# A state-space attention with a gated feed-forward network on one core: wider chunks for the first two pairs, another norm, state additions among the outputs, and a new order of steps

## The chip, the cores and the metric

The kernel runs on one core of one Trainium2 chip. The core has five engines that each work through their own instructions in order and wait for one another by semaphores: TensorE (PE, matrix products; PEld is its loading of weights), VectorE (DVE), ScalarE (ACT), GpSimd (POOL) and SyncE (SP, which here only issues DMA transfers). TensorE reads SBUF and writes PSUM, whose banks the other engines read and free. The metric is the device time of one execution in microseconds (us). All times below are in us.

## The reference

Two operators follow each other. The first is a Mamba-2 state-space scan over x (4 batches, 8 heads, 768 steps, 32 values a head), with a decay a per head and step and with B and C of 16 values. Per head it is a recurrence over chunks of the sequence:

```
log_a = log(clip(a, 1e-6, 1));  cum = cumsum(log_a) within a chunk
L[i,j] = exp(cum[i] - cum[j]) for i >= j, else 0
y      = (C B^T * L) x  +  (C state) * exp(cum)
state  = exp(sum log_a) * state + sum_j exp(cum[-1] - cum[j]) * B_j x_j
```

The result doesn't depend on how long a chunk is, only the work does: the first term of y is inside a chunk (intra-chunk), the second comes from the state before it (inter-chunk).

The heads are put side by side, 3072 tokens of 256 values, and go through the second operator, a feed-forward network without bias:

```
xn  = x / sqrt(mean(x*x) + 1e-6) * rms_g
out = (silu(xn @ w_gate) * (xn @ w_val)) @ w_out        # 256 -> 1536 -> 256
```

All inputs are float32 arrays, and the products are float32 products.

## The kernel before, in words

**Tiling.** The 3072 tokens are six blocks of 512 (numbered 0 to 5). A block is two pairs, so pairs 0 to 11; a pair is two pieces of 128 steps of one batch, in which the scan is worked in chunks of 64, that is four chunks a pair. `NPAIR` is 12, `HC` is 64 (half a piece), `NH` the 8 heads, `NQ` the 4 groups of two heads, `halves` the two chunks of a piece.

**The scan of a pair.** Its steps, by their names in the order and the lines of before.py:

- `bc` and `x` (SP) fetch B, C and x; `scale` (DVE, L449) multiplies them by decays; `turn` (PE, L464) transposes, and `T`, `Tt` (ACT, for pair 0 DVE, L486 and L967 to L970) copy the transposed tiles out of PSUM.
- the decay matrix L: for pairs 0 to 3 `mask`, `sums` (PE, L392 to L409) add the logs up in a pair of PSUM banks and `exp` (ACT, L416) takes the exponential of all 8 heads at once; for later pairs `spread` (SP, L422) writes rows of logs into L by DMA, `sub` (DVE, L428) and `ex` (ACT L434, POOL L436) do the rest. The rows come from `r` (PE, L331) and `parts` (DVE, L338 to L345).
- `g` (PE, L494) is the product of B and C, `L`, `L1` (DVE, L513, L519) multiply it into the decay matrix.
- `A` (PE, L534) is the sum over j in the update of the state, the *additions*; `S` (DVE, L547 to L557) masks them and runs the states on.
- `y` (PE, L574) is the output: the inter-chunk products first, then 64 intra-chunk ones. The result lies in a pair of banks and two single ones, 128 of 512 columns each.
- `sq` (ACT L610, POOL L613) squares it and adds the two halves of features, `yt` (ACT L624, for block 0 DVE L626) copies it out.

**The norm of a block.** `ms` (PE, L636) takes the mean of the squares over features, four small products that leave the tokens on partitions; `mc` (ACT, L642) copies, `mt` (PE, L645) transposes, `rs` (DVE L650, POOL L652) adds 1e-6 and takes the power -1/2, `rb` (PE, L658) transposes four times, so that each token's factor stands on all partitions, and `xn` (DVE, L670, for block 0 L674) multiplies. In block 0 `rc` (ACT, L663) copies the factors to SBUF as `r`.

**The network.** Block 0 begins with plain products: `early` (PE, L703) works on the outputs before they are normed, `norm` (DVE, L714) multiplies by r; `gate` (PE, L693) works on xn; `silu`, `hid` follow, `o` (PE, L809) is the output projection. The rest, from feature tiles 3 to 5 of block 0 on, is done by Strassen's scheme with seven products instead of eight: `P.k.j` (PE, L777, four matmuls of 128x256, 0.86 of PE) is product k of feature tile j, `take` (ACT, L783) copies one of them out of PSUM, `C` (DVE, L789) adds, `silug`, `hidg` or `silu`, `hid` (ACT L798, DVE L802) make the hidden values, `s`, `s2` to `s4` their sums, `O.k.j` (PE, L867) the seven products of the output projection, `Otake` (ACT, L883) and `Oadd` (DVE, L891, L894) combine them, `out` (SP) writes them.

**The weights** come as words of 64-bit floats and are decoded on the core in 20 pieces: `fetch` (SP), `pow` (ACT, L169 to L172), `man` (DVE, L179, L182), `wt` (DVE, L188); `cw`, `tx`, `two` (DVE, L747, L754, L823) make the sums of weights and inputs for Strassen's scheme. Most of that goes on while blocks 0 and 1 are worked.

**What sets the order.** Nothing is scheduled by a program: a string (L1046 to L1207) lists every step as `block:step.numbers/slot`, and a loop (L1208 to L1217) emits the steps in that order. Each step appends its instructions to the engines that it uses, so an engine's queue is the order of the string cut down to that engine, SP's DMA issues and table loads of ACT included. `/slot` names which of three pairs of PSUM banks block 0 uses; `switch` hands two of these over to the network's tiles. `table` asks for an ACT table ahead of its first use. `spread` of a pair needs its L buffer free; there are four (`LBUFS`).

## Time and profile before

| What | us |
|---|---|
| time of the runs, median of 3 | 415.13 (414.54 to 415.45) |
| time of the profiled execution | 414.91 |
| its span, first to last instruction | 413.2 |
| PE busy | 403.3 (98%) |
| DVE busy | 301.0 (73%) |
| ACT busy | 214.8 (52%) |
| POOL busy | 42.3 (10%) |
| mean granted clock of TensorE | 0.996 of full |

The span is what the profile shows; 1.7 of the profiled execution lie around it. "Busy" counts an instruction from its start to its modelled end, and matmuls overlap, so the start of one to the start of the next says what one costs. The parts of the page used below: shares of busy time; the span in 40 slices (a digit is the busy share in tenths); the chain of work that ended last, followed back from the last instruction; groups of instructions by line, operation and tile; the timeline, where consecutive instructions of a kind are put together ("x4"); and busy time by stretch. In a group's or timeline's line `out<-in` names the tiles, and `<-` in the part on idle time names what ended it.

### The profile page before, as it was taken

Reading aid. Unit: us, or ns where it says so; the run is one execution under the profiler, and the core shown is the slowest. Engines: PE = TensorE matmul, PEld = TensorE weight load, DVE = VectorE, ACT = ScalarE, POOL = GpSimd, SP = SyncE. Lnnn points to the kernel's source line nnn. Section 1 sums busy time; section 2 is a strip of 40 time slices with the busy share of each in tenths; the row PEclk is TensorE's granted clock in tenths of the full one; section 3 lists DMA queues with packets and bytes.
Section 4 is the critical chain, followed back from the end, with each engine's and each line's share of the span. In section 5 each row is a group of like instructions: output and inputs, shape, how many; then the busy total and the mean of one; then the engine's idle time right before and its main releaser. Section 6 shows DMA issues by size and latency. Waiting matters only on the chain.

```text
span 413.2 us, 10058 instructions
## 1 busy us (share of the span) xinstructions
PE 403.3 (98%) x4118; PEld 343.2 (83%) x4118; DVE 301.0 (73%) x712; ACT 214.8 (52%) x497; POOL 42.3 (10%) x64
## 2 busy tenths in 40 slices
PE   7789999999999999999999999999999999999997
PEld 5457467888888899888899888899988889988897
DVE  5989999789968878476796465787366876356781
ACT  2869997755656426645362547451556431235410
POOL 2011000012300015000033000012200001000000
PEclk9989999999999999999999999999999999999999
DMA  9979848900111440201070406000100000100001
GB/s 121 255 157 238 208 53 173 203 0 2 39 39 52 92 65 27 78 0 29 12 85 10 78 2 127 2 2 2 52 0 3 1 3 0 52 0 2 1 2 51
DMA packets 87374, 23.95 MB, mean 58 GB/s; under 512 B 76800, under 2 KB 81152, under 8 KB 87328
## 3 DMA queue, kind: packets, MB, share of 16 engines
q1 hardware_dynamic: 83168, 23.05, 26.9%
q10 hardware_dynamic: 4160, 0.26, 1.1%
q8 instruction: 32, 0.52, 0.5%
q14 instruction: 14, 0.11, 0.1%
HBM read 20.02 MB, written 3.28 MB: 56 GB/s over the span
## 4 chain that ended last, share of the span: by engine, by line
PE 90%; DVE 6%; issue 2%; ACT 1%; POOL 0%; DVEq 0%; POOLq 0%
PE gate L777 27%; PE o L867 21%; PE val L777 20%; PE y L574 4%; PE gate L693 3%; PE o L809 3%; PE gate L703 2%; PE g L494 2%; PE tp L464 1%; PE A_ps L534 1%; DVE sw L747 1%; PE rb L658 1%; PE idle L274 1%; DVE L L428 1%; PE ms L636 1%
## 5 line engine op out<-in xcount | busy, mean ns | idle before, releaser
L789 DVE TENSOR_TENSOR c<-val,p 128x512 f32<-128x512 f32 x99 | 67.5, 688 | 41.8 <-PE val L777 33.4
L783 ACT COPY p<-gate 128x512 f32<-128x512 f32 x99 | 57.6, 588 | 69.5 <-PE gate L777 67.6
L777 PE MATMUL gate<-tx,sw 128*128 128x256 f32 x264 | 66.8, 383 | 0.7 <-ACT p L783 0.7
L777 PEld LDWEIGHTS gate<-tx,sw 128*128 128x128 f32 x264 | 48.6, 190 | 8.5 <-ACT p L783 1.4
L798 ACT ACTIVATE c<-c 128x256 f32<-128x256 f32 x99 | 38.4, 417 | 24.6 <-DVE c L789 24.5
L802 DVE TENSOR_TENSOR h<-c 128x256 f32<-128x256 f32 x99 | 41.2, 429 | 10.9 <-ACT c L798 10.9
L777 PE MATMUL val<-tx,sw 128*128 128x256 f32 x132 | 34.1, 383 | 0.4 <-DVE c L789 0.4
L777 PE MATMUL val<-xn,wgv 128*128 128x256 f32 x132 | 33.7, 381 | 0.0
L777 PE MATMUL val<-xn,sw 128*128 128x256 f32 x132 | 33.5, 381 | 0.0
L777 PE MATMUL gate<-xn,wgv 128*128 128x256 f32 x132 | 33.1, 381 | 0.0
L777 PE MATMUL gate<-tx,wgv 128*128 128x256 f32 x132 | 33.0, 384 | 0.0
L613 POOL TENSOR_TENSOR sq<-sq 128x256 f32<-128x256 f32 x12 | 9.1, 760 | 213.6 <-ACT sq L610 187.5
L867 PE MATMUL o<-wo,h 128*128 128x128 f32 x240 | 30.8, 278 | 0.0
L867 PEld LDWEIGHTS o<-wo,h 128*128 128x128 f32 x240 | 28.6, 192 | 1.0 <-issue 0.6
L867 PE MATMUL o<-two,h 128*128 128x128 f32 x240 | 29.3, 275 | 0.0
L867 PE MATMUL o<-two,s 128*128 128x128 f32 x240 | 28.6, 275 | 0.0
L867 PEld LDWEIGHTS o<-two,h 128*128 128x128 f32 x240 | 28.1, 192 | 0.3 <-issue 0.2
L777 PEld LDWEIGHTS val<-tx,sw 128*128 128x128 f32 x132 | 24.5, 190 | 4.3 <-DVE c L789 0.8
L436 POOL TENSOR_SCALAR_AFFINE_SELECT L<-L 64x512 f32<-64x512 f32 x32 | 23.1, 722 | 47.4 <-ACT L L434 45.8
L867 PEld LDWEIGHTS o<-two,s 128*128 128x128 f32 x240 | 27.7, 192 | 0.0
L777 PEld LDWEIGHTS gate<-tx,wgv 128*128 128x128 f32 x132 | 24.5, 190 | 3.8 <-ACT p L783 0.2
L777 PEld LDWEIGHTS val<-xn,sw 128*128 128x128 f32 x132 | 24.7, 190 | 3.5 <-DVE m L179 0.2
(162 smaller groups left out, 651.4 us busy)
## 6 DMA issues: line engine op xcount, KB each, us to landing
L<-rowd SPq DMA_DIRECT2D x32, 128.0 KB, 3.8
xr<-in_x_dram SPq DMA_DIRECT2D x24, 128.0 KB, 4.4
wr<-in_moe_w_out_dram SPq DMA_DIRECT2D x6, 512.0 KB, 5.3
wr<-in_moe_w_gate_dram SPq DMA_DIRECT2D x5, 512.0 KB, 5.8
wr<-in_moe_w_val_dram SPq DMA_DIRECT2D x5, 512.0 KB, 6.9
out_dram<-ob SPq DMA_DIRECT2D x9, 256.0 KB, 2.2
br<-in_B_dram SPq DMA_DIRECT2D x22, 64.0 KB, 4.9
cr<-in_C_dram SPq DMA_DIRECT2D x22, 64.0 KB, 3.7
```

The costliest lines, as they stand in the source:

```text
L436: nc.gpsimd.affine_select(out=L[r], in_=L[r], pattern=[[0, NH], [1, HC]], compare_op=ALU.is_ge, fill=0.0, base=0, channel_multiplier=-1)
L494: nc.tensor.matmul(out=g[u, P * i:P * i + P].rearrange("p (t m) -> p t m", t=2), lhsT=T[r, i, 0, u], rhs=T[r, i, 1:3, u], start=(i == 0), ...
L574: nc.tensor.matmul(out=y[2 * k + u][rows, i * HC:(i + 1) * HC], start=(k, u, rows.start) not in opened, stop=True, skip_group_check=True, ...
L613: nc.gpsimd.tensor_tensor(out=sqs[blk][:, tk], in0=s2[:, 0], in1=s2[:, 1], op=ALU.add)
L693: nc.tensor.matmul(out=gv[:, k], lhsT=w[:, t, fs], rhs=xns[0][:, t], start=(t == 0), stop=(t == 1))
L777: nc.tensor.matmul(out=dst[:, half[w]], lhsT=lhsT, rhs=rhs, start=(k in (1, 2, 5) and w == 0), stop=True, skip_group_check=True)
L783: nc.scalar.copy(out=t, in_=Xs[j])
L789: nc.vector.tensor_tensor(out=t, in0=Zs[j], in1=a, op=ALU.add)
L798: nc.scalar.activation(out=u, in_=src[:, half[0]], func=AF.Silu)
L802: nc.vector.tensor_tensor(out=hidden_tile(blk, j)[:, c // 10 - 1, c % 10 - 1], in0=u, in1=src[:, half[1]], op=ALU.mult)
L809: nc.tensor.matmul(out=o, lhsT=hs_[blk, f // 2][:, f % 2, k // 2, (k % 2) * P:(k % 2 + 1) * P], rhs=wo[:, f], start=opens, stop=(f == NF - ...
L867: nc.tensor.matmul(out=o[t] if apart else o[:, t * P:(t + 1) * P], lhsT=lhsT[:, t], rhs=rhs, start=(k in (1, 2, 4, 5) and j == 0 and (apar ...
```

## The change

**1. Whole chunks for pairs 0 and 1.** A piece of 128 steps is one chunk there. L is a tile of 128 instead of 64 columns a head; `mask`, `sums` and `exp` work on four heads at a time, twice a pair; `g` makes products of 128x256 in two pairs of banks one after the other, and `L` multiplies 128x1024 at a time; the additions and states are two a pair instead of four (one bank); `y` (`first_outputs`) has 24 products of 128 columns, 20 in pair 0, in one pair of banks; `sq` is one, `yt` two instructions. The decays over whole pieces come from three extra small products (in `other_sums`, `chunk_sums`).

**2. Another norm.** `ms` is one product with a 128x128 matrix of 1/256, whose result stands on all partitions at once. `rs` is two ACT instructions: Ln with 1e-6 as bias, then Exp with scale -1/2, which write r to SBUF. `mc`, `mt`, `rb`, `rc` and the power on POOL are gone; `xn` reads r.

**3. Additions in the outputs' tile group.** At the end of `y` of pairs 2 to 10 the additions of the next pair are written into free columns of y's pair of banks. Those of pairs 0, 1 and 2 keep their own step.

**4. Buffers.** L has two buffers instead of four.

**5. The order.** The string of steps is a new one throughout. The number of steps of each kind of the network's products is as before (962 matmul instructions of the network in both programs). Tables that ACT loads: 25 in the program after, 13 before. A step can ask for filler products (`*n`); no step of the order does.

The core of the diff (the string of the order is left out):

```diff
...
-    Ls, LBUFS = {}, 4
+    Ls = {}
...
-        if g // 2 not in Ls:
-            Ls[g // 2] = ssd.tile([P, 2, NH, HC], FP32, tag="L", name="L", bufs=LBUFS)
-        return Ls[g // 2][:, g % 2]
+        p = g // 2
+        if p not in Ls:
+            Ls[p] = ssd.tile([P, 2, NH, P if p < 2 else HC], FP32, tag="L", name="L", bufs=2)
+        return Ls[p][:, g % 2]
...
-    def decay(p, e):
+    def decay(p, half, e):
         pair_tile(2 * p)
-        nc.scalar.activation(out=Ls[p].rearrange("p i h m -> p i (h m)"), in_=e, func=AF.Exp)
+        L = Ls[p][:, :, 4 * half:4 * half + 4] if p < 2 else Ls[p]
+        nc.scalar.activation(out=L.rearrange("p i h m -> p i (h m)"), in_=e, func=AF.Exp)
...
+                if p < 2:
+                    nc.tensor.matmul(
+                        out=g[:, 256 * i:256 * i + 256], lhsT=T[r, i, 0],
+                        rhs=T[r, i, 1:3].rearrange("p t m -> p (t m)"),
+                        start=(i == 0), stop=True, tile_position=(32 * q, 0),
+                        skip_group_check=True)
+                    continue
...
-    def additions(p):
+    def additions(p, A_ps=None):
         s = st[p]
-        ps["A", p] = A_ps = [bank("A_ps", (P, 2, 2, D)) for u in range(2)]
+        if A_ps is None:
+            A_ps = [bank("A_ps", (P, 2, 2, D)) for u in range(1 if p < 2 else 2)]
+        ps["A", p] = A_ps = A_ps if p >= 2 else 2 * A_ps
         for i, u in chunks_of(p)[2]:
+            r = slice(0, P) if p < 2 else halves[u]
             for q in range(NQ):
                 nc.tensor.matmul(
                     out=A_ps[u][32 * q:32 * q + 32, i].rearrange("p t d -> p (t d)"),
-                    lhsT=s["Bd"][halves[u], i, 2 * q:2 * q + 2].rearrange("p t n -> p (t n)"),
-                    rhs=s["x"][halves[u], i, 2 * q:2 * q + 2].rearrange("p t d -> p (t d)"),
-                    start=(i == 0), stop=True, tile_position=(HC * u, 32 * q),
+                    lhsT=s["Bd"][r, i, 2 * q:2 * q + 2].rearrange("p t n -> p (t n)"),
+                    rhs=s["x"][r, i, 2 * q:2 * q + 2].rearrange("p t d -> p (t d)"),
+                    start=(i == 0), stop=True, tile_position=(r.start, 32 * q),
                     skip_group_check=True)
...
+    def first_outputs(p, y):
+
+        s = st[p]
+        ps["y", p] = y
+
+        def inter(i, opens):
+            S, CdT = state[2 * (2 * p + i) - 1], s["T"][:, i, 3]
+            for q in range(NQ):
+                r = slice(32 * q, 32 * q + 32)
+                o = 64 * (q % 2)
+                nc.tensor.matmul(
+                    out=y[o:o + 64, q // 2, i * P:(i + 1) * P],
+                    lhsT=S[r].rearrange("p t d -> p (t d)"), rhs=CdT[r],
+                    start=opens, stop=True, tile_position=(32 * q, o),
+                    skip_group_check=True)
+
+        def intra(i, opens):
+            for h in range(NH):
+                o = 32 * (h % 4)
+                nc.tensor.matmul(
+                    out=y[o:o + 32, h // 4, i * P:(i + 1) * P], lhsT=s["x"][:, i, h],
+                    rhs=Ls[p][:, i, h], start=opens, stop=True,
+                    tile_position=(0, o), skip_group_check=True)
+
+        if p:
+            inter(0, True)
+        intra(0, p == 0)
+        intra(1, False)
+        inter(1, False)
+        del st[p], Ls[p]
...
     def outputs(p, y):
 
+        if p < 2:
+            return first_outputs(p, y)
...
+        if 2 <= p < NPAIR - 1:
+            additions(p + 1, [y[u][:, P:2 * P].rearrange("p (i t d) -> p i t d", i=2, t=2)
+                              for u in range(2)])
         del st[p], Ls[p]
...
+        if p < 2:
+            sq2 = nrm.tile([P, 2, 256], FP32, tag="sq2", name="sq2", bufs=1)
+            nc.scalar.activation(out=sq2, in_=ps["y", p][:, :, 0:256], func=AF.Square)
+            nc.gpsimd.tensor_tensor(out=sqs[blk][:, tk], in0=sq2[:, 0], in1=sq2[:, 1], op=ALU.add)
+            return
...
-        ps["m", blk] = ms = bank("ms", (P, 2, P))
-        for k in range(NT):
-            nc.tensor.matmul(out=ms[32 * k:32 * k + 32, 0], lhsT=mean32,
-                             rhs=sqs[blk][:, k * P:(k + 1) * P], start=True, stop=True,
-                             tile_position=(0, 32 * k), skip_group_check=True)
+        ps["m", blk] = ms = bank("ms", (P, TB))
+        nc.tensor.matmul(out=ms, lhsT=mean, rhs=sqs[blk], start=True, stop=True)
...
-    def norm_back(blk):
-        nc.tensor.transpose(out=ps["m", blk][:, 1], in_=ps.pop(("mr", blk)), identity=ident)
...
     def norm_roots(blk):
-        me = nrm.tile([P, NT], FP32, tag="me", name="me")
-        ms = ps.pop(("m", blk))[:, 1].rearrange("p (k r) -> p k r", r=32)[:, :, 0]
-        nc.vector.tensor_scalar_add(me, ms, 1e-6)
-        ps["rs"] = rs = nrm.tile([P, NT], FP32, tag="rs", name="rs")
-        nc.gpsimd.tensor_tensor(out=rs, in0=me, in1=nhalf, op=ALU.pow)
-
-    def norm_turn():
-        rs = ps.pop("rs")
-        ps["rb"] = rb = bank("rb", (P, NT, P))
-        for k in range(NT):
-            nc.tensor.transpose(out=rb[:, k], in_=rs[:, k:k + 1].to_broadcast([P, P]),
-                                identity=ident)
...
+        ps["r", blk] = r = nrm.tile([P, TB], FP32, tag="sq2", name="r", bufs=1)
+        nc.scalar.activation(out=r, in_=ps.pop(("m", blk)), func=AF.Ln, bias=eps)
+        nc.scalar.activation(out=r, in_=r, func=AF.Exp, scale=-0.5)
...
```

## The prediction

> **What bounds the kernel.** Times are in us unless marked. I read the page first (busy shares, slices, the chain that ended last, by engine):
>
> ```profile
> PE 403.3 (98%) x4118; PEld 343.2 (83%) x4118; DVE 301.0 (73%) x712; ACT 214.8 (52%) x497; POOL 42.3 (10%) x64
> ...
> PE   7789999999999999999999999999999999999997
> ...
> DVE  5989999789968878476796465787366876356781
> ...
> PE 90%; DVE 6%; issue 2%; ACT 1%; POOL 0%; DVEq 0%; POOLq 0%
> ```
>
> PE is at 9 tenths from the fourth slice to the last but one and is 90% of the chain. So time is won only by fewer or cheaper PE instructions, by an earlier first FFN product, or by removing a wait of PE. FFN work can't shrink: both programs have 962 FFN matmuls. Then I read the stretches, where DVE and ACT could be the limit (columns: busy PE, PEld, DVE, ACT, POOL with counts; clock, DMA share, GB/s):
>
> ```profile
> 20.00:40.00 20.00, 18.04 (x287) 12.78 (x270) 17.39 (x42) 16.44 (x34) 2.64 (x3) 0.91 0.83 187
> 40.00:60.00 20.00, 19.65 (x205) 11.04 (x206) 19.66 (x42) 18.60 (x37) 0.85 (x1) 1.00 0.66 144
> ```
>
> From 20 to 60 DVE (17.4 and 19.7 of 20) and ACT (16.4, 18.6) are nearly as full as PE: they decode weights there. Next the chain in order of time (start, length): what starts block 0's FFN, and the few links that are not PE's.
>
> ```profile
> 23.11 2.10 PE y L574 x95
> 25.21 2.98 PE gate L703 x8
> ...
> 37.81 3.63 PE gate L693 x8
> ...
> 223.88 1.03 POOL rs L652
> ...
> 235.92 1.28 ACT L1044
> ```
>
> Then PE's timeline around an addition of block 1:
>
> ```profile
> 114.83 1.03 PE L777 MATMUL val<-xn,wgv 128*128 128x256 f32 x4
> 115.79 0.45 PE L534 MATMUL A_ps<-xr,Bd 64*32 64x64 f32 x32
> 116.17 1.13 PE L777 MATMUL val<-xn,wgv 128*128 128x256 f32 x4
> ```
>
> Last, the groups of PE by shape (records | busy, mean ns of one | idle before and its releaser):
>
> ```profile
> L693 PE MATMUL gate<-xn,wgv 128*128 128x512 f32 x32 | 14.5, 599 | 0.0
> ...
> L658 PE MATMUL rb<-ident,rs 128*128 128x128 f32 x24 | 3.6, 275 | 0.2 <-POOL rs L652 0.2
> L636 PE MATMUL ms<-sq,mean 128*32 128x128 f32 x48 | 2.6, 285 | 0.0
> L645 PE MATMUL ms<-ident,mr 128*128 128x128 f32 x6 | 1.7, 282 | 0.0
> ```
>
> A matmul's own mean overlaps the next one's; what counts is from start to start. In the timeline four products at 0.216 from 114.83 would hand over at 115.69, and the next starts at 116.17: 0.48. Measured so over all visits: the additions of one pair (24 or 32 records) hold FFN work up by 0.45 to 0.48, of which first to last start is 0.21 to 0.24, and the next product is 0.10 later still; inside y the 64 intra-chunk records take 0.64 to 0.79, 10 to 12 ns each. One norm holds PE up by ms 0.45 + 0.10, mt 0.11, rb 0.44: 1.10. A full 128x512 fp32 pass (L693) is 0.43 from start to start.
>
> [...] The trace shows 1.283 a load (13 of them), but 1.29 to the next instruction[...]; I use 1.29. [...] The changed program has two loads there all the same (25 in all): Ln and Exp each bring their own in norms 1 to 5; only block 0's norm runs under the combined set loaded at the start.
>
> **Part 1: prologue and block 0 (first FFN product to the first Strassen product).** Whole chunks of 128 halve A and the intra-chunk matmuls of pairs 0 and 1 but double the decay data. By instruction, for both pairs: four multiplies of 128x1024 instead of 128x512, 1.14 instead of 0.60 from start to start (nearest row xn L674, 1.139): DVE +2.2. Two exps more of 128x1024 on ACT, 0.90 each: +1.8. State updates 4 fewer at 0.31, masking of A 2 fewer at 0.20, y's copy 0.2 less: DVE -1.8. PE: y.0 and y.1 have 20 and 24 matmuls of 128 columns instead of 88 and 96 records (1.4 to 1.5 each). Everything of the set-up that DVE does stands ahead of the clipped logs (4.8 before, about 5.4 after). Laying the steps end to end by these durations, each on its engine after its inputs: the row parts end at 9.1 (8.7); the first exp needs only half the sums, so 10.8 (11.3); L at 14.3 to 15.4, 16.1 to 17.2, 18.0 to 19.1, 21.3 to 22.5, y.1 at 22.5 (23.1), first early product at 25.0 (25.2): no difference so far.
>
> What differs is the norm. Before, it goes ms 29.96, copy, mt, DVE, POOL pow (1.2), rb only at 33.13, since a block of products stands before it on PE; copy; r at 35.0:
>
> ```profile
> 29.96 0.43 PE L636 MATMUL ms<-sq,mean 128*32 128x128 f32 x8
> ...
> 31.52 1.19 POOL L652 TENSOR_TENSOR rs<-me,nhalf 128x4 f32<-128x4 f32 x1 [4.89 <-DVE me L650]
> ...
> 34.38 0.64 ACT L663 COPY r<-rb 128x512 f32<-128x512 f32 x1
> ...
> 35.05 1.22 DVE L674 TENSOR_TENSOR xn<-yt,rb 128x1024 f32<-128x1024 f32 x1 [0.26 <-ACT r L663]
> ```
>
> After: ms about 27.6 to 28.5, Ln and Exp 0.53 each behind what ACT holds, r at 30.1. xn can't use that: it waits for DVE's queue. From the end of yt.0 (24.95, for it waits on the square of y.0) DVE holds four mantissas (three of 1.07, one small of 0.66: 3.9), four weights (2.1), the parts of a row (1.3), scaling (0.7), yt.1 (0.8), two products with r (1.2) and xn (1.14): 11.1, so 36.0 (36.2 before). Of the 5 that r gains, none is left. But on PE g of pair 2 (0.72) now stands after the first full gate product, and turns of pair 3 (0.33) before: gate.2 at 36.1 (37.8), gate.3 40.3 (41.7), first Strassen product 51.9 (52.8). y.2 with A.3 ends at 54.8; the next product waits 0.55 for the hidden tile 5 on DVE; y.3 now carries A.4 and so waits for pair 4's x, whose transfer SP issues only behind y.2 (its median to landing is 4.4: about 59 to 60), and ends at 62.0 (64.3). I take 2.0 ahead. Bounds: 4.5 ahead and 0.5 behind, 2.5 to each side, since a single displaced decode (pow 2.2 + man 1.1 + wt 0.6 = 3.9) moves DVE's and ACT's queues by more than that.
>
> **Part 2: the additions in y's tile group.** Nine go there, pairs 3 to 11; pairs 3 and 4 are in part 1's clock, seven remain. No own visit: 0.45 to 0.48 + 0.10 goes and 32 records at 10 to 12 ns, 0.32, come: 0.26 each. Bounds: 0.10 [...] and 0.34 (records at the first-to-last 0.24). Seven x 0.26 = 1.8. The masked copy and state updates on DVE (L547, L557) are then queued behind y instead of ahead of it; the y that needs them stands some ten products later (at 0.86, about 9), so this costs nothing; without that cover, the 2 x 0.20 + 4 x 0.31 = 1.6 would be PE's wait.
>
> **Part 3: norms 1 to 5.** ms becomes one fp32 matmul of 128x512 with a 128x128 mean: 2 passes x 0.43 = 0.86, for 1.10: 0.24 x 5 = 1.2. No run shows it in this place, but L693 is its shape. DVE loses the small add, POOL the pow. ACT gains Ln + Exp 2 x 0.53 and two loads 2 x 1.29, loses a copy: about 3.4 a norm, 2.6 of them loads. What is queued behind on ACT: the copy Otake and take (L783), for which PE's next product in that bank waits. From PE's queue: block 1 to 2, Otake ready 3.6 after ms, PE comes to its bank at 3.9; 2 to 3, 0.9 in hand; 3 to 4, rs stands behind Otake.7, a turn waits 0.65 for its bank and the next block's first product 0.45 for xn: 1.1; 4 to 5 none; at the end of block 0, DVE is ready 9 after P.5.5, PE's cover is 11.7. If the cover were gone each would cost up to 2.6.
>
> **Part 4: old and new waits of the order.** Before, PE waits 0.55 at 107.9 (DVE chain of combined weights), 0.4 at 224 (POOL's pow) and 0.55 at 237.4 (take behind a table load): 1.5, with 0.4 in small ones. Those go. In their place: 1.1 from part 3, and 0.8 for waits that I can't see by hand. Net 0, bounds 1.5 either way. Other new: two L buffers for four. The transfers that spread the log rows into L (SP; 3.8 to landing) then wait for the y two pairs earlier, and with them whatever SP has behind them (x, B, C, outputs). They are placed behind that y in the order, with about a pair's products, 30, to the L that they serve: nothing; without the cover, 3.8 plus DVE's and ACT's passes on them once a pair. The tail is the same sequence of products, adds and output.
>
> **Sum**, against the profiled execution, 414.9 (span 413.2 and 1.7 around it; the runs' median is 415.1): 413.2 - 2.0 - 1.8 - 1.2 - 0 = 408.2; + 1.7 = 409.9, called 410.0.
>
> **Rivals.** *The prologue's lead doesn't last* (DVE full to 60, wide multiplies on it): part 1 gives 0, 412.0. For it: 98% DVE in 40 to 60; against: its sum of work hardly changes (+0.3). *The merge doesn't pay*: records cost the same inside y as outside (bound 0.10): 1.1 less, 411.1, inside my own range. *Slower: ScalarE's table loads become PE's wait.* Twelve more loads are 15.5 of ACT, most beside takes. Place: the products after each of five norms; price up to 2.6 each, when Otake or the next block's take stands behind Ln and Exp with no cover. It decides from 1.2 a norm on: 410.0 without the 1.1 counted already, 408.9, + 5 x 1.2 = 414.9. I put its time at 1.5 a norm, 416.4; all five at 2.6 would be 421.9. For it: take did wait behind a load, at 235.9; my cover at block 1 is 0.3 alone. Against: three of five have more. *The change doesn't do what it says*: additions are written into y's columns 128 to 256 in the order of the program, so excluded for them; the filler does nothing, as no step asks for it.
>
> **Chances.** Likeliest, 407.6 to 412.0 around 410.0: 0.68. More gained (prologue 4.5 instead of 2.0, no new wait instead of 1.9), 405.6 to 407.6: 0.09. Waits eat most of it (412.0 to 414.3): 0.09. No change: 0.04. Slower by the loads: 0.10. 0.2% (0.8) is what a measurement can tell from nothing. So faster 0.86, same 0.04, slower 0.10. The range 406.2 to 414.6 takes in the bounds of the four parts and leaves out the slower case and the end of the larger gain, some 0.13; the likeliest alone has 407.6 to 412.0.
>
> **What would show it.** y longer by 0.2 to 0.4 and no L534 group outside it from block 1 on; ms of 0.86 with no L645 or L658; r at 30 and gate.2 near 36; 25 loads; the first product after pair 3's y near 62. Wrong, if PE waits on ACT takes after norms for more than 1 each, if gate.2 comes after 37.8, or if DVE's decoding makes PE wait at the end of block 0.

## The result: slower, where a gain was forecast

| | median | range | runs |
|---|---|---|---|
| before | 414.54 | 412.13 to 417.11 | 17 |
| changed | 417.52 | 415.35 to 420.54 | 17 |

The ratio is 1.0062, with a 95% interval of 1.0035 to 1.0089: the change costs about 2.6 us. The forecast was 410.0, 406.2 to 414.6. The profiled execution of the changed kernel took 416.64, with a span of 414.9 (1.7 around it, as before). Medians here and below are of fast runs; a single run, of 418.60 in experiment 5, was slow and is not counted.

First the page of the changed kernel: busy shares, PE's row of the 40 slices, and the chain by engine.

```profile
PE 403.1 (97%) x3870; PEld 342.3 (83%) x3870; DVE 302.5 (73%) x698; ACT 237.7 (57%) x512; POOL 40.4 (10%) x61
...
PE   8989989999999999999999999999899999999997
...
PE 79%; DVE 10%; ACT 7%; issue 2%; DMA 1%; POOL 0%; DVEq 0%; POOLq 0%; ACTq 0%
```

PE is busy as long as before (403.3), in 248 fewer matmuls. ACT has 23 us more, of which 15.4 are the 12 further table loads (1.283 each, as before). The chain tells most: PE had 90% of it and has 79%; DVE, ACT and a DMA took the rest. Work went away from PE, and PE waits instead. Its list of waits says where (waiting line, what it waited for: total, times, longest):

```profile
PE y L656 <- ACT T L1034: 1.7, 1, 1.7
PE gate L844 <- DVE ob L961: 1.4, 1, 1.4
...
PE tp L499 <- ACT r L729: 0.9, 1, 0.9
PE A_ps L582 <- ACT T L1034: 0.9, 1, 0.9
...
PE gate L844 <- DVE xn L737: 0.5, 1, 0.5
```

Before, no single wait of PE after the first 50 us passed 0.5 in this list. Two of the five lie in the prologue (A.2 at 46.4 and y.2 at 57.1), three at the norms of blocks 2 and 3. Four of the five have two causes, which the experiments below take apart: y.2 waits behind weights that land late, the three at the norms behind loads of ACT's tables. The wait at 46.4 is neither; it stays until experiment 6 moves these additions.

What was forecast of PE's own work came out. The groups of the changed kernel by shape (records | busy, mean ns):

```profile
L725 PE MATMUL ms<-sq,mean 128*128 128x512 f32 x12 | 6.2, 602 | 0.0
L582 PE MATMUL y<-xr,Bd 64*32 64x64 f32 x264 | 5.1, 226 | 0.0
```

A norm is two passes (12 records for six norms); from the last product before to the next after it they take 0.86 beyond the products, as forecast. The additions of nine pairs now write into y. PE's timeline of the changed kernel at one of them:

```profile
144.33 0.69 PE L656 MATMUL y<-T,S 32*64 32x64 f32 x32
144.96 0.80 PE L656 MATMUL y<-L,xr 64*32 64x64 f32 x60
...
145.61 0.54 PE L582 MATMUL y<-xr,Bd 64*32 64x64 f32 x30
146.08 0.71 PE L934 MATMUL o<-wo,h 128*128 128x128 f32 x4
```

The additions run on without a pause after y's last products, and the next product of the network starts 0.47 after the first of the last thirty. Counted as the own visits were, from the end of the products before it by their usual distance, this visit takes 1.84; a y alone took up to 1.50, an own visit of the additions up to 0.48, and 0.10 after it: 2.08. So this pair saves 0.24. Over the seven visits from block 1 on it is 0.24 to 0.30, 0.27 in the mean (0.26 forecast).

To see where the gain went, I subtract from the start of each matmul of the network the price of all network matmuls ahead of it (0.216, 0.112 and 0.429 each, 335.0 in all). What is left is all that isn't network work, up to there: the lower, the better. The first two columns of times are the two kernels; the last three are experiments told below.

| network work done | before | changed | fetch by use | one table | fetch by use, one table |
|---|---|---|---|---|---|
| 0 (first early product) | 25.14 | 25.46 | 25.46 | 25.59 | 24.57 |
| 8 (first gate product) | 30.93 | 30.18 | 30.18 | 30.30 | 29.28 |
| 24 (around y.2) | 34.72 | 38.17 | 36.12 | 36.39 | 35.22 |
| 32 (after y.3) | 39.48 | 43.13 | 41.49 | 40.96 | 41.28 |
| 192 (block 3 under way) | 63.01 | 62.58 | 60.95 | 58.76 | 59.10 |
| 232 (start of block 4) | 67.59 | 70.53 | 68.91 | 65.01 | 65.37 |
| 334 (end) | 75.25 | 76.99 | 75.37 | 71.47 | 71.82 |

The changed kernel starts even. Its lead of 0.75 at the first gate product isn't the order's doing: the kernel before takes 2.98 for its first eight early products, with its clock at half from 23.9 to 27.3, and 1.73 for the next eight. It then falls 3.65 behind by the row after y.3, has made up 4.1 by block 3, and loses 3.4 of that again at the norms of blocks 2 and 3 and until block 4 starts, against a before that has waits of its own there. In sum: additions 9 x 0.27 = 2.4 and norms 5 x 0.24 = 1.2 gained; single waits of PE over 0.25 from 40 on (a start later than the usual distance from the one before) are 7.0 instead of 2.3, so 4.7 lost; 0.3 later start: about 1.4, where the span is 1.7 longer. Waits under 0.25 aren't in this count.

### The profile page after: what moved, and what is told of

Same layout as the page of the kernel before. It is cut to its first block, busy times and chain, and to the rows that moved or that the text cites. A ratio compares the mean times of both kernels' runs of the same rounds, so it can differ in the third digit from the quotient of the medians.

```text
span 414.9 us, 9585 instructions
## 1 busy us (share of the span) xinstructions
PE 403.1 (97%) x3870; PEld 342.3 (83%) x3870; DVE 302.5 (73%) x698; ACT 237.7 (57%) x512; POOL 40.4 (10%) x61
## 4 chain that ended last, share of the span: by engine, by line
PE 79%; DVE 10%; ACT 7%; issue 2%; DMA 1%; POOL 0%; DVEq 0%; POOLq 0%; ACTq 0%
PE gate L844 25%; PE o L934 20%; PE val L844 19%; PE y L656 3%; PE o L876 2%; PE gate L760 2%; PE tp L499 1%; PE g L536 1%; DMA wr<-in_moe_w_gate_dram 1%; PE gate L770 1%; DVE sw L814 1%; ACT e L183 1%; ACT e L182 1%; DVE xn L737 1%; PE ms L725 1%
## 5 line engine op out<-in xcount | busy, mean ns | idle before, releaser
L844 PE MATMUL gate<-tx,sw 128*128 128x256 f32 x264 | 65.4, 383 | 0.2
L869 DVE TENSOR_TENSOR h<-c 128x256 f32<-128x256 f32 x99 | 40.6, 423 | 16.1 <-ACT c L865 16.1
L471 POOL TENSOR_SCALAR_AFFINE_SELECT L<-L 64x512 f32<-64x512 f32 x32 | 26.3, 823 | 75.5 <-ACT L L469 73.9
L844 PE MATMUL val<-tx,sw 128*128 128x256 f32 x132 | 33.2, 380 | 0.1
L934 PE MATMUL o<-two,s 128*128 128x128 f32 x240 | 29.8, 275 | 0.0
L934 PE MATMUL o<-wo,h 128*128 128x128 f32 x240 | 29.7, 275 | 0.0
L844 PEld LDWEIGHTS gate<-xn,wgv 128*128 128x128 f32 x132 | 24.3, 190 | 5.9 <-DVE ob L961 1.6
L950 ACT COPY v<-o 128x256 f32<-128x256 f32 x15 | 5.6, 372 | 40.0 <-PE o L934 39.9
L934 PE MATMUL o<-two,h 128*128 128x128 f32 x240 | 28.4, 275 | 0.0
```

The lines of the kernel that those rows point to most:

```text
L471: nc.gpsimd.affine_select(out=L[r], in_=L[r], pattern=[[0, NH], [1, HC]], compare_op=ALU.is_ge, fill=0.0, base=0, channel_multiplier=-1)
L844: nc.tensor.matmul(out=dst[:, half[w]], lhsT=lhsT, rhs=rhs, start=(k in (1, 2, 5) and w == 0), stop=True, skip_group_check=True)
L869: nc.vector.tensor_tensor(out=hidden_tile(blk, j)[:, c // 10 - 1, c % 10 - 1], in0=u, in1=src[:, half[1]], op=ALU.mult)
L934: nc.tensor.matmul(out=o[t] if apart else o[:, t * P:(t + 1) * P], lhsT=lhsT[:, t], rhs=rhs, start=(k in (1, 2, 4, 5) and j == 0 and (apar ...
L950: nc.scalar.copy(out=ts[k], in_=halves_of(Os["X"]))
```

## The experiments

### 1. Which queue makes y.2 wait

y.2 waits for ACT's copies of pair 3's transposed tiles. The timeline of the changed kernel shows what these stood behind:

```profile
44.29 0.52 SPq L160 DMA_DIRECT2D wr<-in_moe_w_val_dram  x1
...
48.28 0.76 ACT L182 ACTIVATE e<-wr,kinks 128x512 int16<-128x512 int16 x1 [1.91 <-DMA wr<-in_moe_w_val_dram]
...
51.36 0.79 ACT L182 ACTIVATE e<-wr,kinks 128x512 int16<-128x512 int16 x1 [0.82 <-DMA wr<-in_moe_w_gate_dram]
...
56.21 0.35 ACT L1034 ACTIVATE T<-tp,tmask 128x128 f32<-128x128 f32 x1
...
57.14 0.56 PE L656 MATMUL y<-T,S 32*64 32x64 f32 x20 [1.66 <-ACT T L1034]
```

SP issues the transfer of weight piece 9 at 44.29 and it lands at 48.25; ACT stands idle for 1.91 with the decoding of that piece at the head of its queue, again 0.82 for the next one, and the copies come behind both, at 56.2. y.2 writes into banks that these copies free. In the kernel before, piece 9 is decoded from 44.1 on, here from 48.3. In the new order pieces 11, 15 and 18 are fetched early, and B and C of later blocks stand ahead of 9 and 10 on SP. The trace shows SP's queue as what holds piece 9: SP issues without a pause up to it, and two of the issues ahead, of B, take 2.33 and 2.39 each. The three early pieces also hold three of the six buffers for weights until they are decoded (11 to 54.8, 15 to 78, 18 to 91.9); that this delayed piece 9 isn't shown.

The first repair exchanges pieces 9 and 10 for 15 and 18 on SP. These are the steps that move, each with its neighbours:

```diff
-0:x.3 0:pow.5 0:fetch.15 0:man.1
+0:x.3 0:pow.5 0:fetch.9 0:man.1
...
-0:man.4 0:fetch.18 0:exp.3
+0:man.4 0:fetch.10 0:exp.3
...
-0:man.6 0:fetch.9 0:wt.4
+0:man.6 0:fetch.15 0:wt.4
...
-0:pow.8 0:wt.8 0:fetch.10 0:silu.1
+0:pow.8 0:wt.8 0:fetch.18 0:silu.1
```

> The changed kernel with four transfers exchanged in the order: pieces 9 and 10 of the weights are fetched where pieces 15 and 18 were, and the other way round. Theory (fetch order): pieces 9 and 10 stand behind B and C of later blocks on SP and are decoded 4 us later than before, and ACT's copies of pair 3's transposed tiles queue behind that decoding, so y.2 waits 1.9. Then pow.9 no longer waits for its transfer, y.2's wait falls below 0.7, and the time falls by 1.5 to 2.5. Rival (ACT's order alone: the copies stand behind two pow whenever these start): y.2 still waits 1.4 or more and the time falls by less than 0.5.

Measured: 417.14 (416.72 to 418.26), no faster by the medians. All four runs have a mean clock of 0.992 or 0.996; beside the changed kernel's runs at 0.996 (417.9), those at 0.996 (417.1) are 0.8 faster. But the wait of y.2 is gone, as the theory had it: piece 9 is decoded at 46.3, the copies end at 54.2, y.2 runs through from 55.0. What came in its place is in the timeline of this experiment:

```profile
61.70 0.43 DVE L192 TENSOR_SCALAR m<-wr 128x512 int32<-128x512 int32 x1 [1.82 <-DMA wr<-in_moe_w_val_dram]
...
62.77 0.69 DVE L556 TENSOR_TENSOR L<-g,L 128x512 f32<-128x512 f32 x1
...
63.51 1.35 PE L656 MATMUL y<-T,S 32*64 32x64 f32 x24 [2.10 <-DVE L L556]
```

The same thing one piece later: piece 13 was still late, DVE stood 1.82 at the head of its queue for it, and the multiply into L that y.3 needs was behind. Right behind this wait the clock is at half from 64.1 to 67.5 (see the last section). So the theory was right on the mechanism and wrong on the price of one repair; the rival (the copies are late in any case) falls.

So all pieces were put in the order in which they are decoded, on the same places of the order (the fetch steps alone, in their order, before and after the edit):

```diff
-fetch 0 1 2 3 4 5 11 6 7 8 15 18 9 12 10 14 13 16 19 17
+fetch 0 1 2 3 5 4 6 7 8 9 10 11 12 13 14 16 15 17 18 19
```

> The changed kernel with its 20 weight transfers put in the order in which ACT decodes them, at the same places of the order, so that no piece holds one of the six buffers long before it is decoded. Theory (late transfers: in the changed order pieces 9, 10 and 13 land only as they are wanted, and what queues behind their decoding on ACT and DVE makes y.2 and y.3 wait): pieces 9 to 13 are decoded without a wait for a transfer over 0.5, y.2 and y.3 wait less than 0.7 together instead of 2.7, the first product after y.3 comes 2 or more earlier, and the runs lie closer together; time 414 to 415.5. Rival (ACT and DVE are simply full there): the waits move to another step and the time falls by less than 0.7.

Measured: 414.60 (413.63 to 415.35, 12 runs), 2.9 below the changed kernel; against before 0.9995 (0.9979 to 1.0011). Pieces 9 to 13 are decoded at 46.2, 48.4, 51.1, 55.5 and 60.1 and y.2 doesn't wait. The column of the table says where: level with the changed kernel at the first gate product, 2.05 ahead at y.2 and 1.6 from y.3 to the end. That is the profiled execution. Runs at full clock say the same: ten of the changed kernel have a median of 416.1, all twelve of this one 414.6, so 1.5. The other 1.4 of the medians' 2.9 is that seven of the changed kernel's runs had a lower clock and none of these; the last section comes back to it. The runs lie within 1.7 of each other instead of 5.2.

### 2. The table loads at the norms

The chain of the changed kernel from the norm at the end of block 2 into block 3 (start, length):

```profile
219.95 0.64 ACT L L469
...
220.60 1.28 ACT L729
...
221.90 0.69 ACT r L729
...
222.61 1.28 ACT L730
...
223.90 0.64 ACT r L730
...
224.56 1.85 DVE xn L737 x2
...
227.87 1.00 DVE ob L961 x3
...
228.92 1.99 PE gate L844 x8
```

Ln and Exp take 1.33 and their two loads 2.56. xn, the sums of inputs for Strassen's scheme and three additions of outputs follow on DVE, and only the last of these frees the bank that the next product needs.

Block 0's norm has no loads between: ACT's timeline of the changed kernel shows Ln, Exp and an exponential of decays one behind the other, and no load from the one at 0.78 (line 323, the combined set) to the one at 37.01.

```profile
30.03 0.69 ACT L729 ACTIVATE r<-ms,eps 128x512 f32<-128x512 f32 x1 [0.79 <-PE ms L725]
30.75 0.63 ACT L730 ACTIVATE r<-r 128x512 f32<-128x512 f32 x1
31.32 1.02 ACT L451 ACTIVATE L<-e 128x1024 f32<-128x1024 f32 x1
```

The repair asks for this set ahead of the other norms too (`set`). The steps that change, without those between:

```diff
-0:rs.1
+0:set 0:rs.1
...
-0:ex.11
+0:set 0:ex.11
...
-1:ex.0
+0:set 1:ex.0
...
-2:ex.0
+0:set 2:ex.0
...
-3:ex.3
+0:set 3:ex.3
...
-4:rs
+0:set 4:rs
...
-0:table.0
-0:table.1
-2:table
```

> The changed kernel with the combined table of logarithm and exponential asked for ahead of each norm and the idle requests for Silu's table taken out: 14 loads instead of 25. Theory (the loads make PE wait at the norms): the waits of 1.55 at 228.9 and of 1.1 and 0.65 at 291 to 294 fall to 0.7 together, the time by 2 to 3. Rival (PE waits there for the row of additions and combined inputs on DVE, whatever ACT does): each wait keeps more than half, the time falls by less than 1.

Measured: 414.90 (411.13 to 416.94, 20 runs), 2.6 below the changed kernel. The same chain in the profiled execution of this experiment, which took 411.13:

```profile
217.37 0.64 ACT L L469
218.01 0.58 ACT r L729
...
218.61 0.64 ACT r L730
...
219.28 2.08 DVE xn L737 x2
...
223.98 1.08 DVE ob L961 x3
...
225.10 1.99 PE gate L844 x8
```

With the combined set L's exponential, Ln and Exp start at 217.37, 218.01 and 218.61, with no load between them where the changed kernel has two of 1.28. From L to xn it takes 1.9 instead of 4.6, and the wait of 1.55 is 0.3; the two at 291 and 294 are gone altogether. The rival falls, although it saw something: DVE's row is still the end of this chain.

These runs fall into two groups: seven with a mean clock of 0.999 or more and a median of 411.7, thirteen at 0.992 to 0.996 and 414.0 to 416.9. The profiled one is of the first group, and in it y.2 doesn't wait, although the order is the changed kernel's in all that stands ahead of y.2:

```profile
46.72 0.77 ACT L182 ACTIVATE e<-wr,kinks 128x512 int16<-128x512 int16 x1 [0.24 <-DMA wr<-in_moe_w_val_dram]
...
55.07 0.85 PE L656 MATMUL y<-T,S 32*64 32x64 f32 x32
```

SP came to piece 9 at 42.16 instead of 44.29, since its issues ahead of it were shorter, and the piece landed at 46.70 instead of 48.25, though its transfer took longer (4.5 for 4.0). So whether y.2 waits differs from one execution of this order to the next. By the table 2.2 of the 5.5 that this profile gains were won by the row after y.3; the norms give the other 3.3.

The two causes together:

> The same with the combined table too (14 loads). If the two causes are separate, the gains add: 2.6 and 2 to 3 below the changed kernel, 411.5 to 412.5 in the median, below the kernel before by 2 to 3. If the transfers are not the cause, it stays at 414.5 to 415.

Measured: 411.05 (410.77 to 411.48, 6 runs), ratio to before 0.9912 (0.9889 to 0.9936). By medians 2.9 and 2.6 forecast 412.0, and this kernel is 0.95 below that. In runs at full clock the gains don't add: 1.5 and 4.4 alone, 5.1 together, where the profiled run with one table hadn't the wait of y.2 to lose. It was run again beside another one:

> The kernel with the transfers in order of use and the combined table once more, for a comparison with the one beside it: 411.0, runs within 1 of each other. If the narrow spread of its first six runs was chance, runs of 413 and more with a mean clock of 0.996 turn up as they did with the combined table alone.

410.83 (409.83 to 412.90, 6 runs), ratio 0.9907 (0.9872 to 0.9941). One run of the six has 412.9 and a mean clock of 0.996, so such runs are rare, not excluded.

### 3. The norm alone, in the kernel before

If loads are what cost, the new norm should cost in the old order too. The norm was put there alone (`ms` one product, `rs` as Ln and Exp at the old place of the roots, `mc`, `mt`, `rb`, `rc` out):

```diff
-        ps["m", blk] = ms = bank("ms", (P, 2, P))
...
+        ps["m", blk] = ms = bank("ms", (P, TB))
+        nc.tensor.matmul(out=ms, lhsT=mean, rhs=sqs[blk], start=True, stop=True)
...
+        nc.scalar.activation(out=r, in_=ps.pop(("m", blk)), func=AF.Ln, bias=eps)
+        nc.scalar.activation(out=r, in_=r, func=AF.Exp, scale=-0.5)
```

> The kernel before with the new norm alone (one product with a 128x128 matrix, Ln and Exp on ACT at the place of the old roots), 24 table loads instead of 13. Theory (the norm is cheaper on PE but pays with loads where ACT has no room): PE's gaps for the norm fall from 1.1 to 0.86 each, the wait for POOL of 0.4 at 225 goes, and waits for ACT of 1 to 2.6 appear at one or two of the norms: the time within 1.5 of before on either side. Rival (the norm itself is the gain that was forecast, 1.2 and 0.4): 1.6 faster with no new wait over 0.3.

Measured: 423.45 (420.52 to 424.94), 9.0 slower than before, far outside both. Its chain at the norm of block 1:

```profile
83.10 1.28 ACT L638
...
84.40 0.69 ACT r L638
...
86.40 0.63 ACT r L639
87.03 1.28 ACT L774
...
91.51 0.48 ACT p L759
...
92.03 1.22 PE gate L753 x2
```

Three loads (1.28 for each of the two that the chain shows whole), ahead of Ln, Exp and then Silu, hold ACT for 5.2 with the two operations; PE waits 2.5 at 90.0 and 1.1 at 92.0 for what stands behind. Two more waits follow at 167 to 172 (0.9 and 1.6) and one at 237 (1.1). Part of the rest is PE's clock: in this execution it was at half from 20 to 30 and from 92 to 95, mean 0.983 (0.992 in the other three runs).

With the combined table set there as well (`0:set` ahead of `rs` or the first `ex` of each block):

> The kernel before with the new norm and the combined table (17 loads instead of 24). Theory (the loads were what cost): the waits at 90, 172 and 236 fall below 1 each and the time comes to 415 to 417, about that of before. Rival (the order of before has no room for the new norm on ACT and DVE whatever the loads): within 2 of the 423.5 without it.

Measured: 418.62 (417.06 to 421.50), 4.8 better with 7 loads fewer, but still 4 slower than before: the waits at 85 (1.2), 87 (1.1) and 161 to 166 (0.9 and 1.6) remain. So the loads are about half of it. The other half I read from the waits that remain: the old order has no room for this norm, and an operation that moves from POOL to ACT needs the order rebuilt around it. That is argued; no run shows it. The wait of 1.6 behind a turn didn't move with the loads; I didn't follow it further.

### 4. What an own visit of the additions costs

First try: additions of pairs 3 to 11 issued one product behind y, into the same columns, each state step directly behind its additions. The theory: an own visit costs the pause around it, 0.45 to 0.48 for 0.24 of starts, and 0.10 after it. The rival: inside y the same pause comes back elsewhere.

```diff
-            additions(p + 1, [y[u][:, P:2 * P].rearrange("p (i t d) -> p i t d", i=2, t=2)
-                              for u in range(2)])
+            room[p + 1] = [y[u][:, P:2 * P].rearrange("p (i t d) -> p i t d", i=2, t=2)
+                           for u in range(2)]
...
-1:y.1 1:hid.11.4 1:hid.22.4 1:hid.21.4 1:C.12.4 1:silu.12.4 1:O.1.0 1:O.5.0
+1:y.1 1:hid.11.4 1:hid.22.4 1:hid.21.4 1:C.12.4 1:silu.12.4 1:O.1.0 2:A.0 2:S.0 1:O.5.0
```

> The changed kernel with the additions of pairs 3 to 11 taken out of y and issued behind the next product of the network, into the same columns. Theory [...]: 0.26 a pair more, nine pairs, 2.3 in all, the gaps of y shorter by 0.32 and nine new gaps of 0.45 to 0.6. Rival [...]: 1 or less.

Measured: 437.04 (433.45 to 439.90), 19.5 slower. That isn't the pause of the visits. Their gaps are as in the kernel before (0.45 and 0.48; y 1.50 or less), but there are new single waits of 2.5, 1.9, 1.2, 2.4 and 3.5, and the list of waits of this experiment names DVE's sums first:

```profile
PE val L844 <- DVE c L856: 6.8, 4, 3.3
```

A state step that waits at the head of DVE's queue for the later additions holds up the sums behind it, and PE's products wait for those. The experiment moved two things, and the second was the larger. Two of the three waits over 2, at 57 and at 287, were also followed by half clock, the one at 205 wasn't (see the last section).

Second try, in the faster kernel (fetch by use, one table): the additions of pairs 5 to 11 one product *ahead* of y, so that nothing on DVE changes its place. Theory and rival are the same two; the rival has 0.5 or less if the pause comes back elsewhere, 10 and more if the visits were what made the first try slow.

```diff
+    def additions_ahead(p):
+        if p < 5:
+            return additions(p)
+        ready[p - 1] = y = pair_of_banks("y", 2)
+        additions(p, [y[:, u, P:2 * P].rearrange("p (i t d) -> p i t d", i=2, t=2) for u in range(2)])
...
-1:P.2.4 1:silu.12.2 1:y.0
+1:A.1 1:P.2.4 1:silu.12.2 1:y.0
```

> The kernel with the transfers in order of use and the combined table (411.05), and in it the additions of pairs 5 to 11 taken out of y and put one product of the network ahead of it, into the same columns, so that the states and everything else on DVE keep their places. Theory [...]: seven own gaps of 0.45 to 0.48 and 0.10 after, y shorter by 0.32: 0.26 x 7 = 1.8 slower, 412.9. Rival ([...]the 21 us of the run with the additions behind y came from the visits): 0.5 or less, or 10 and more.

Measured: 412.82 (411.77 to 413.01, 15 runs), 1.77 slower than 411.05, where 1.8 was expected: 0.25 a pair. The two ran on different chips; set against the kernel before that ran beside each, the difference is 1.2 to 1.5, and the profiled spans differ by 1.5 to 1.9. So 0.2 to 0.27 a pair. The timeline of this experiment shows a visit with its pause (0.46 of matmuls, the product behind it 0.39 after its start):

```profile
140.26 1.13 PE L850 MATMUL val<-xn,sw 128*128 128x256 f32 x4
141.32 0.46 PE L582 MATMUL y<-xr,Bd 64*32 64x64 f32 x32
141.71 0.48 PE L850 MATMUL val<-xn,sw 128*128 128x256 f32 x1
```

### 5. The whole chunks

> The same kernel (411.05) with chunks of 64 in pairs 0 and 1 too, as in all others; a few steps of the start had to be moved for their banks (the outputs' copies ahead of the next pair's, the additions of pair 0 and two sums of rows later). Theory (whole chunks are worth nothing on the path, as DVE and ACT set the time of the start): first gate product within 1 of 36.1 and the time 410 to 412.5. Rival (whole chunks are what keeps the start short): 2 to 4 slower, with y.0 and y.1 of 1.4 to 1.5 each instead of about 1 and the first product of the network 2 or more later.

The edit, in the faster kernel: every `p < 2` of the scan's steps takes the branch for chunks of 64, and `0:middles` stands where `0:mids` was. Because that needs more single banks, `yt` of pairs 0 and 1, `A.0`, `row.0`, `row.1` and `r.1` had to be moved by some steps.

Measured: 414.52 (411.54 to 416.58, 19 runs), 3.5 slower than with whole chunks, about the size that the rival gave. The first gate product starts at 43.0 instead of 36.2. But some of it is the moved steps (the additions of pair 1 wait 2.4 at 19.3), and some is PE's clock, which is at half in much of the first 36 us (mean of the execution 0.984). How much is the chunks' own stays open: they need fewer banks, and without that the order of the start can't be kept.

### 6. Two repairs that brought nothing

The additions of pair 2 wait 1.1 at 46.4 for copies of the transposes just ahead. They were put behind the next gate product:

```diff
-0:man.9 0:A.2 0:S.2 0:pow.9
+0:man.9 0:pow.9
...
-0:gate.4/2
+0:gate.4/2 0:A.2 0:S.2
```

> The same, and the additions of pair 2 and their states stand behind the gate product 4 instead of between the transposes of pair 3 and it. The wait of 1.1 of these additions for ACT's copies goes: 1 below the kernel without it, if nothing else on the path takes its place; 0 if the decoding on ACT and DVE sets the time of the next steps anyway.

Measured: 413.95 (413.02 to 415.94, 12 runs), 2.9 slower than without. The wait at 46.4 went, and the transposes of pair 3 then waited for the banks of the additions, whose reading (line L596) stood behind decoding on DVE: 3.2 in the list of waits.

```profile
PE tp L499 <- DVE A L596: 3.2, 1, 3.2
```

The other one takes the additions of pair 4, which wait for a late x, out of y.3:

```diff
-        if 2 <= p < NPAIR - 1:
+        if 2 <= p < NPAIR - 1 and p != 3:
...
-0:y.3/2 1:S.0 0:yt.3
+0:y.3/2 0:yt.3
...
-0:P.4.3 0:P.3.3 0:cw.4
+0:P.4.3 1:A.0 0:P.3.3 0:cw.4 1:S.0
```

> The kernel with the transfers in order of use and the combined table, and in it the additions of pair 4 alone taken out of y.3 and put three products of the network behind it. In the trace of the kernel without this edit, y.3 waits 1.3 to 1.5 for pair 4's x, which SP can issue only after y.2. Theory (that wait is on the path): it goes, an own visit of 0.26 comes, 1 faster in an execution like the profiled one, 0.5 to 1 in the median. Rival (DVE and ACT decode weights there and set the pace in any case): within 0.3 either way, with the wait back at a later step.

Measured: 411.09 (410.22 to 411.39, 6 runs) beside 410.83. The wait was 1.5 in the first trace of the kernel without this edit and 0.4 in the second; it went, and the own visit (0.26) and a wait of 0.5 at 71.9 took its place. The rival holds.

## Why the prediction was wrong, step by step

**Part 1, prologue (2.0 ahead forecast): the step that failed.** Up to the first gate product the laying out of steps held: first exp 10.5 (10.8 forecast), multiplies into L at 14.8, 16.6, 18.7, 22.0 (14.3, 16.1, 18.0, 21.3), first early product 25.5 (25.0), gate.2 37.1 (36.1). That gate.2 is ahead of before (37.7) is luck, by the table: before lost about 1.25 there to a half clock. The working left it out, though the prediction's row of 20 to 40 has a clock of 0.91. From there "first Strassen product 51.9" was 54.0, of which 1.1 is the wait of the additions of pair 2, which I had costed without one. "y.2 with A.3 ends at 54.8" was 58.7, and "the next product waits 0.55 for the hidden tile 5" was a wait of 1.9 in y.2 itself, for ACT. y.3 ended at 65.9 where 62.0 was forecast and before had 64.3. At equal work of the network that is 2.4 behind before at the end of y.3, and 3.65 at the table's row after it, where 2.0 ahead was forecast.

I had laid every step on PE, DVE, ACT and POOL after its inputs, and taken each weight as landed when its decoding came up. Of SP I followed one transfer, pair 4's x. Whether a piece lands in time depends on SP's row, which is in the order of `fetch` steps, and that I never compared (9 and 10 stood behind 11, 15 and 18). The run with the fetches in order of use shows that cause: 2.05 in the profile at y.2, 1.6 from y.3 on. The wait of the additions of pair 2 is another 1.1. What is left of the difference isn't taken apart; work of the scan that the new order does earlier can be part of it.

I gave 2.5 to each side of this part because "a single displaced decode moves DVE's and ACT's queues by more than that". That was the right kind of risk with too small a size: the part was 4.4 to 5.65 off.

**Part 2, additions.** 0.26 a pair; the trace says 0.24 to 0.30, 0.27 in the mean, and the run with seven of them taken out 0.2 to 0.27. The bound of 0.10 (inside y the pause comes back elsewhere) is excluded; what PE does in the pause isn't shown. That the state steps behind y cost nothing held as well; the failed first try shows what they cost where they do wait.

**Part 3, norms.** PE: 0.86 for 1.10, to the hundredth. ACT: no wait at block 0 to 1, 1 to 2 and 4 to 5, as forecast; at 3 to 4, 1.1 forecast and 1.76 measured; at 2 to 3, "0.9 in hand" was a wait of 1.55, the second step that failed. There I had asked when ACT comes to `Otake`, and not what stands behind xn on DVE: four sums of inputs and three additions of outputs, whose last reading frees the bank of the product. The chain shows them: 2.5 from the end of xn to the start of the product. That the loads were the reason is shown by the run with the combined table.

**Part 4.** I set the waits that go against 1.1 + 0.8 new ones: net 0, within 1.5. The old ones were 2.3 in all; the new ones were 7.0, so this term was about 4.7. The waits are those of parts 1 and 3, seen as a sum. The range took these risks for smaller than the parts had them: the bounds that parts 1, 2 and 4 give, added on one side, come to 415.1, outside it; the measured 417.5 is outside of both.

**The rivals.** The slower one had its mechanism right (loads between the norm and the next block) and its price too high for each of five norms; it came to 3.3 at two of them. Alone it would not have made the kernel slower: with the transfers repaired and the loads left as they were, the kernel equals before, and so it does with the loads repaired and the transfers left (0.9995 and 0.9994). Each cause eats about half of what the change gains on PE; I had given the sum of both no chance of its own. *The prologue's lead doesn't last* was the other half, again with another engine at its root: not DVE's work, but SP's order. What the whole chunks are worth, to which part 1 gave no difference, stays open (experiment 5).

## What to carry to other kernels

An order written by hand is the program of every queue, and the DMA queue is one of them: lay the transfers out too, with the buffers that they hold and until when, before any engine is given its steps. When an operation moves to ACT, count its table loads (1.28 each here) and follow what stands behind the result on the next engine, up to the read that frees PE's bank. A gain on the bounding engine is only as good as the waits that it leaves: ask of each one, in order, what is late next.

## What the runs showed of the hardware that I had not expected

In the run with A.2 behind gate.4 a pause of PE cost twice. PE is idle from 49.4 to 52.5, and these are its stretches of one us each (PE, PEld, DVE, ACT, POOL busy; then the granted clock):

```profile
50.00:51.00 1.00, 0.00 (x0) 0.00 (x0) 0.97 (x3) 0.97 (x3) 0.00 (x0) 1.00 1.07 414
51.00:52.00 1.00, 0.00 (x0) 0.00 (x0) 1.00 (x2) 1.00 (x3) 0.00 (x0) 0.75 1.05 404
52.00:53.00 1.00, 0.45 (x2) 0.46 (x3) 0.96 (x5) 0.94 (x3) 0.00 (x0) 0.50 1.12 325
...
57.00:58.00 1.00, 1.00 (x2) 0.34 (x1) 0.00 (x0) 0.00 (x0) 0.00 (x0) 0.50 0.86 86
58.00:59.00 1.00, 1.00 (x3) 0.38 (x2) 0.00 (x0) 0.00 (x0) 0.00 (x0) 0.83 0.85 191
```

About 2 us into the pause, at 51.5, the clock halves and stays so to 58.3 (0.75 and 0.83 are half and a third of a us at half rate): 6.83, well after PE is busy again: gate products of 0.43 take 0.85, six of them in a row, 2.5 on top of the pause of 3.2. PE had been fully idle for 2.1 when the clock fell. In the kernel before half rate lasted 3.41, half as long. In the run with the additions behind y there are two such stretches, again of 6.83, at 57.4 and at 286.1; at the second PE had been idle for 1.7. A pause of 2.2 at 204.8 in the same run cost no clock: the two stretches alone make up its mean of 0.984. So these runs give no length of pause that is safe, and don't show what sets the length of the half rate.

The kernel before has such a stretch in its start: in its profiled execution the clock is at half from 23.9 to 27.3, after waits of 1.5 (before the sums at 21.7) and 0.5. That is where its first eight early products take 2.98 and the next eight 1.73. Of the 23 runs of before beside the first experiments, 22 have a mean clock of 0.992 to 0.996. The one left, and one more beside the later experiments, had full clock and took 416.0 each, not less, so what this stretch costs the whole kernel isn't shown.

The changed kernel's runs differ in this: ten of the 17 have a mean clock of 0.999 or more and a median of 416.1, four have 0.996 and 417.9, three 0.992 and 420.0. That fits its wait in y.2, which differs from one execution to the next with the moment at which SP comes to piece 9 (44.29 here, 42.16 in experiment 2), and which is gone in the profile with the fetches by use; all 12 runs of that kernel have a clock of 0.999 or more. A case of such a wait with half clock right behind it is the wait of 2.1 in the profile of the first swap in experiment 1 (64.1 to 67.5). For the changed kernel itself the link is argued, not shown: only one execution of it was profiled, and that one had the wait of 1.9 and full clock.
